# Fewer and larger weight loads, four selector and cast moves, and a permute on ScalarE in a fused attention and feed-forward kernel

## The chip, the cores and the metric

The kernel runs on one core of a Trainium2 chip. The metric is device time in microseconds (us): the median of repeated runs. Beside the runs there is one profiled execution, whose trace is read here. Engines are named as the profile names them: PE (TensorE matmul), PEld (its weight loads), DVE (VectorE), ACT (ScalarE), POOL (GpSimd), SP (SyncE). L145 is line 145 of the kernel.

## The reference

Inputs are q, k, v of shape [4 batches, 8 heads, 768 tokens, 64], a matrix `sort_net` [4, 8, 8, 8], and the weights of a feed-forward layer: w_in [512, 2048], w_out [2048, 512] and two scalars s and b. All are float32.

```
P = sort_net
repeat 5 times:                       # Sinkhorn
    P = exp(P - rowmax(P)); P = P / (rowsum(P)+1e-9); P = P / (colsum(P)+1e-9)
k_sorted[i] = sum_j P[i,j] * k[block j]     # 8 blocks of 96 tokens; the same for v
attn = softmax(q_block @ k_sorted_block^T / 8)
x    = attn @ v_sorted_block                # heads side by side: [3072, 512]
out  = (s * relu(x @ w_in)^2 + b) @ w_out
```

## The kernel before

The work goes batch by batch. The tokens of a batch are split into two halves of four blocks, so that eight tiles of 384 tokens pass through the feed-forward part: `ffn1` (L482, x @ w_in, 64 matmuls a tile, with relu on ACT and the square on DVE) and `ffn2` (L514, @ w_out). The order of every engine is written out by hand: the program is issued in one order, and `slots` of `ffn1` and `ffn2` name the attention pieces of the next batch that are issued between their matmuls. `k_piece` (L288) and `v_piece` (L372) mix the blocks with a matrix built from P. A k piece uses the loaded keys as weights. A v piece needs the values with token and feature dimension exchanged: `permute` (L184) writes them to the tile VP, [128, 64 features, 64], and a v piece reads 16 features of it.

**Start.** SP loads sort_net and batch 0's v as four float32 chunks `v0f` (L83). PE runs 160 matmuls on zeros, 110 columns wide (`warm`, L209). Meanwhile DVE and ACT run the Sinkhorn rounds (L210 to L225): exp on ACT, then a row sum, reciprocal, product, column sum, reciprocal, product on DVE (L216 to L224). Behind each exp from the second on, ACT casts and permutes one chunk of v0f into VP (L213), and in rounds 1 and 2 DVE fills its wait for the exp with a mask reduction (`idle`, L199). PE then spreads P over the partitions with the selector `emat` (`pe`, L236): GpSimd makes emat with a memset of all four batches (L131), a select for batch 0 (L132) and two for batches 1 to 3 (L172). For batch 0, DVE builds the mixing matrix `pd` (L255 to L268). For batches 1 to 3 the spread values are kept in PB, copied by ACT (L551). Three k pieces, four v pieces and the scores of batch 0 follow.

**GpSimd's queue.** All loads that change type are issued by GpSimd, in program order: batch 0's keys (L93) and the first half of its q tokens (L111), then `load_w` (L140). That one first copies one element of pd (L148), which makes the queue wait until pd is there, issues two parts of w_in, copies one element of the third key piece's result `ks` (L151) as a second gate, and issues the rest: 16 parts of w_in in all, each 128 rows by 512 columns, with the second half of q between them, and four parts of w_out (L165). Memsets follow (L580 to L586), then the two scalars (L588), and batch 1's loads: k and v in two halves each (`load_z`, L100) and q in eight parts. A load also waits until the load eight places before it has landed, since the two share a semaphore. Last come five copies of `permute` (L594), 8 features each, for features 0 to 39 of batch 1; DVE does features 40 to 63 in one copy, issued behind `make_bias` in slot 7 of `ffn1(1)` (L634).

**Where batch 1's values are used.** In `ffn2(0)` (L668), three k pieces stand in slot 2, three v pieces in slot 5 and the last in slot 9, all evicted by ACT and DVE in turn.

Of the kernel before, what the change touches and what calls it, by code (L numbers as in the profile page):

```python
# [12 lines left out]
ALU = mybir.AluOpType  # L13
# [3 lines left out]
def spread(t, dims):  # L17

    return bass.AP(tensor=t.tensor, offset=t.offset, ap=[list(t.ap[0])] + dims)
# [3 lines left out]
def kernel(  # L23
# [12 lines left out]
    nc = tc.nc  # L36

    B, H, S, D = q.shape
    NB = sort_net.shape[-1]
    BLK = S // NB  # L40
    BH = B * H
    NHP = H // 2
# [3 lines left out]
    HB = NB // 2  # L46
# [33 lines left out]
    v0f = gtp.tile([128, C2, D], FP, tag="gt", name="v0f")  # L80
    CV = C2 // 4
    for c in range(0, C2, CV):
        nc.sync.dma_start(out=v0f[:, c:c + CV, :].rearrange("p c d -> p (c d)"),  # L83
                          in_=raw[2][0][:, c * D:(c + CV) * D])

    RAW = {}
# [18 lines left out]
    def load_q(b, ns=range(NB)):  # L105

        if b not in QTOK:
            QTOK[b] = rawp.tile([BLK, NB, H, D], BF, tag="rawq", name="qtok")
        qv = q[b].rearrange("h (n t) d -> t n h d", n=NB)
        for n in ns:  # L110
            nc.gpsimd.dma_start(out=QTOK[b][:, n], in_=qv[:, n])  # L111
# [5 lines left out]
    KS = [const.tile([128, NG, 2, GAP], BF, name=f"ks{i}") for i in range(2)]  # L117
# [9 lines left out]
    ident = const.tile([128, 128], BF)  # L127
    make_identity(nc, ident)
    idv = ident.rearrange("p (a e j z) -> p a e j z", a=NHP, e=2, j=NB)
    emat = const.tile([BH, B, 128], FP)  # L130
    nc.gpsimd.memset(emat, 0.0)  # L131
    nc.gpsimd.affine_select(out=emat[:, 0], in_=emat[:, 0], pattern=[[-1, H], [0, 2 * NB]], base=0,  # L132
                            channel_multiplier=1, compare_op=ALU.not_equal, fill=1.0)
    load("k", 0, 3)
    load_q(0, range(HB))
    ones = const.tile([128, 32], BF)
    wi = const.tile([128, NHP, d_ff], BF)
    wo = const.tile([128, NF, d_model], BF)

    def load_w():  # L140
        wiv = moe_w_in.rearrange("(a p) f -> p a f", p=128)
        fq = d_ff // 4

        def part(a, f0, f1):
            nc.gpsimd.dma_start(out=wi[:, a, f0 * fq:f1 * fq], in_=wiv[:, a, f0 * fq:f1 * fq])  # L145


        nc.gpsimd.tensor_copy(out=ones[:, 0:1], in_=PD[0][:, 0, 0, 0:1])  # L148
        part(0, 0, 1)
        part(1, 0, 1)  # L150
        nc.gpsimd.tensor_copy(out=ones[:, 0:1], in_=KS[0][:, 0, 0, C2 - 1:C2])  # L151
        part(0, 1, 2)
        part(1, 1, 2)
        for c in (0, 1):
            for a in (2, 3):
                part(a, c, c + 1)
            if c == 0:
                load_q(0, range(HB, NB))
        for c in (2, 3):
            for a in range(NHP):  # L160
                part(a, c, c + 1)
        wov = moe_w_out.rearrange("(f p) n -> p f n", p=128)
        for c in range(4):
            fs = slice(c * (NF // 4), (c + 1) * (NF // 4))
            nc.gpsimd.dma_start(out=wo[:, fs, :], in_=wov[:, fs, :])  # L165
# [1 line left out]
    nc.gpsimd.memset(VS[0][:, :, D:VW], 1.0)  # L167
    nc.gpsimd.memset(VS[0][32:GAP, :, D:VW], 0.0)
    nc.gpsimd.memset(VS[0][32:C2, :, D:VW], 1.0)
    for z in range(2):  # L170
        em = emat[:, 1:B, z * 64:(z + 1) * 64]
        nc.gpsimd.affine_select(out=em, in_=em, pattern=[[-H, B - 1], [-1, H], [0, NB]], base=-H,  # L172
                                channel_multiplier=1, compare_op=ALU.not_equal, fill=1.0)
    Z = []

    def warm(n, w=512):
        for _ in range(n):
            if not Z:
                Z.append(psb.tile([128, 512], FP, tag="b", name="z"))
            nc.tensor.matmul(out=Z[0][:, 0:w], lhsT=zeros[:, 0:128], rhs=zeros[:, 0:w],  # L180
                             start=True, stop=True)


    def permute(eng, src, cs=slice(0, C2), ds=slice(0, D)):  # L184
        o, i = VP[:, ds, cs], src[:, cs, ds].rearrange("p c d -> p d c")
        if eng is nc.scalar:
            eng.copy(out=o, in_=i)  # L187
        else:
            eng.tensor_copy(out=o, in_=i)  # L189
# [11 lines left out]
            out=jsel, in_=ident.rearrange("p (h j z) -> p j h z", h=H, j=NB), axis=AX.XY, op=ALU.add),  # L201
        lambda: nc.vector.tensor_reduce(
            out=bm.rearrange("p (e z a) -> p e z a", e=2, z=2),
            in_=idv.rearrange("p a e j z -> p e z a j"), axis=AX.X, op=ALU.add),
    ]
    nc.vector.tensor_reduce(out=rstat, in_=sn, axis=AX.X, op=ALU.max)
    nc.vector.tensor_tensor(out=sn, in0=sn, in1=rstat.broadcast_to([BH, NB, NB]),
                            op=ALU.subtract)
    warm(160, 110)  # L209
    for it in range(5):  # L210
        nc.scalar.activation(out=sn, in_=sn, func=AF.Exp)
        if it >= 1:
            permute(nc.scalar, v0f, slice((it - 1) * CV, it * CV))  # L213
        if it in (1, 2):
            idle[it - 1]()
        nc.vector.tensor_reduce(out=rstat, in_=sn, axis=AX.X, op=ALU.add)  # L216
        nc.vector.reciprocal(out=rrec, in_=rstat)
        nc.vector.tensor_tensor(out=sn, in0=sn, in1=rrec.broadcast_to([BH, NB, NB]), op=ALU.mult)
        if it == 4:
            break  # L220
        nc.vector.tensor_reduce(out=rstat, in_=sne.rearrange("p i j -> p j i"),
                                axis=AX.X, op=ALU.add)
        nc.vector.reciprocal(out=rrec, in_=rstat)
        nc.vector.tensor_tensor(out=sn, in0=sn, in1=spread(rrec, [[0, NB], list(rrec.ap[1])]),  # L224
                                op=ALU.mult)  # L225

    PD = {}
    PT = const.tile([128, B, NB], FP)
    RC = const.tile([128, B], FP)
    PB = const.tile([128, B - 1, NB, NB], FP)  # L230
# [283 lines left out]
    def ffn2(t, slots):  # L514
        gt = GT.pop(t)
        last = t == 2 * B - 1
        for m in range(TG // 128 - int(last)):
            ops = psb.tile([128, d_model], FP, tag="b", name="ops")
            for f in range(NF):
                nc.tensor.matmul(out=ops, lhsT=gt[:, f, m * 128:(m + 1) * 128],  # L520
                                 rhs=wo[:, f, :], start=(f == 0), stop=(f == NF - 1))
                if f % 4 == 3:
                    if f == NF - 1:
                        store(t, m, ops)
                    for p in slots.get(m * 4 + f // 4, ()):
                        p()
        if last:
            m = TG // 128 - 1
            h = d_model // 4
            for n0, n in ((0, 2 * h), (2 * h, h), (3 * h, h)):  # L530
                ns = slice(n0, n0 + n)
                ops = psb.tile([128, n], FP, tag="b", name="ops")
                for f in range(NF):
                    nc.tensor.matmul(out=ops, lhsT=gt[:, f, m * 128:(m + 1) * 128],  # L534
                                     rhs=wo[:, f, ns], start=(f == 0), stop=(f == NF - 1))
                store(t, m, ops, ns)
# [11 lines left out]
    take_p(0, 1, spread_p(0, 1), jsel)  # L548
    build_pd(0)
    pe = spread_p(1, B - 1)  # L550
    nc.scalar.copy(out=PB, in_=pe)  # L551
    warm(3)
    k_piece(0, 0, "A")
    k_piece(0, CK, "D")
# [35 lines left out]
    load_z("k", 1)  # L590
    load_z("v", 1)
    load_q(1)
    for i in range(5):
        permute(nc.gpsimd, RAW["v", 1], ds=slice(i * 8, (i + 1) * 8))  # L594


# [56 lines left out]
    for b in range(B):  # L653
        n = b + 1
        if b:
            ffn1(2 * b, {0: [VR_(n, 0, "AD"), VR_(n, 1, "D")],
                         2: [VR_(n, 2, "AD"), lambda: v_back(n), load_qg(n)]} if n < B else {})
        if b:
            ffn1(2 * b + 1, {})
        if n < B:  # L660
            q_dma(n)
        if n == B:
            ffn2(2 * b, {})
            ffn2(2 * b + 1, {})
            break
        K3 = [K(n, 0, "A"), K(n, 1, "D"), K(n, 2, "A")]
        if n == 1:
            ffn2(2 * b, {2: K3,  # L668
                         5: [V(n, 0, "D"), V(n, 1, "A"), V(n, 2, "D"), load_vk(2)],
                         9: [V(n, 3, "D"), SC(n, 0, 0), SC(n, 0, 1)],  # L670
                         11: [P(n, 0, 0), SC(n, 0, 2), SC(n, 0, 3)]})
            ffn2(2 * b + 1, {0: [P(n, 0, 1)], 1: [P(n, 0, 2)],
                             2: [P(n, 0, 3), TD(n, 0), SC(n, 1, 0), SC(n, 1, 1)],
                             4: [P(n, 1, 0)], 5: [P(n, 1, 1), SC(n, 1, 2), SC(n, 1, 3)],
                             7: [P(n, 1, 2)], 8: [P(n, 1, 3), TD(n, 1)]})
        else:
            ffn2(2 * b, {2: K3, 7: [SC(n, 0, 0), SC(n, 0, 1)] + ([load_vk(3)] if n == 2 else []),
                         9: [SC(n, 0, 2), SC(n, 0, 3)]})
            ffn2(2 * b + 1, {0: [P(n, 0, 0), P(n, 0, 1)],
                             2: [P(n, 0, 2), P(n, 0, 3), TD(n, 0)],  # L680
                             3: [SC(n, 1, 0), SC(n, 1, 1)], 4: [SC(n, 1, 2), SC(n, 1, 3)],
                             6: [P(n, 1, 0), P(n, 1, 1)],
                             8: [P(n, 1, 2), P(n, 1, 3), TD(n, 1)]})
# [30 lines left out]
```

## Time and profile before

| what | us |
|---|---|
| median of 4 runs | 226.13 (225.97 to 226.39) |
| profiled execution, its own time | 227.47 |
| its span in the trace | 225.7 |
| PE busy | 217.2 |
| DVE busy, ACT busy, POOL busy | 111.7, 100.1, 60.2 |
| granted TensorE clock | 1.00 in every stage |

Line 1 of the page gives each engine's busy time. The chain is the work that ended last, followed back from the last instruction, at each step to what released it. In the timeline a line is: start, length, engine, line of code, operation, output<-inputs, shape, count; a bracket at its end is the engine's idle time before it and what ended it. In a table by stage (windows), the columns are the stretch and its length, the busy time of the chosen engine, the granted clock, the DMA engines' share and the GB/s that they moved.

Some rows that the next sections use (us):

| row | start | length |
|---|---|---|
| ACT cast of a v0f chunk, L187, four of them | 5.02, 6.63, 8.59, 10.60 | 1.55, 1.53, 1.51, 1.50 |
| ACT exp of the last round, L211 | 10.21 | 0.26 |
| ACT copy of PB, L551 | 12.43 | 0.32 |
| DVE pd, L268 | 12.67 | 0.35 |
| first key pieces on PE, L293 | 13.08 | 1.71 |
| first two key evictions by ACT, L282 | 13.82 | 2.03 |
| first w_in part issued, L145 | 13.65 | lands after 3.8 |
| GpSimd's eight w_in issues behind q | 21.58 | 4.70 |
| last w_out part issued, L165 | 32.27 | lands after 13.2 |
| batch 1's last v part issued, L100 | 41.76 | lands after 14.66 |
| DVE permute of batch 1, L189 | 56.51 | 1.18 |

### The profile page before, as it was taken

The page shows a single profiled execution, that of the slowest core. Times are in us where ns is not written, and L with a number is a line of the kernel's source. Part 1 is how long each engine was busy: PE and PEld are TensorE (multiplying, and loading weights), DVE is VectorE, ACT ScalarE, POOL GpSimd, SP SyncE. Part 2 cuts the span into 40 slices and gives each one's busy share as a digit, 9 for nine tenths or more (in the row PEclk, how much of TensorE's full clock was granted, in tenths as well). Part 3 has the DMA queues.
Part 4 walks back from the last instruction along what each step waited for, and adds up shares of the span by engine and source line. Part 5 has one row for each costly group of instructions (what it writes and reads, how often), then busy time and mean ns, then how long its engine had stood idle before and what let it go on. Part 6 is the DMA issues. An engine that isn't in the chain of part 4 may idle for free.

```text
span 225.7 us, 5487 instructions
## 1 busy us (share of the span) xinstructions
PE 217.2 (96%) x2360; PEld 128.8 (57%) x2360; DVE 111.7 (49%) x232; ACT 100.1 (44%) x131; POOL 60.2 (27%) x101
## 2 busy tenths in 40 slices
PE   8897999999799999999999999999999999999993
PEld 8885656655355555555545545656455566554453
DVE  6747467571746657443318556343425743441222
ACT  4977476565124506655351326664345046550000
POOL 8539679643940006400040009100000000000000
PEclk9999999999999999999999999999999999999999
DMA  5999999989989946997949859969913240001212
GB/s 174 251 104 121 140 178 180 201 181 150 122 179 220 213 125 126 153 120 163 231 94 189 217 163 132 158 63 210 189 77 78 104 119 0 1 0 49 93 46 93
DMA packets 66872, 30.51 MB, mean 135 GB/s; under 512 B 57568, under 2 KB 62048, under 8 KB 66656
## 3 DMA queue, kind: packets, MB, share of 16 engines
q0 software_dynamic: 30960, 12.85, 47.5%
q1 hardware_dynamic: 35888, 17.31, 32.4%
q8 instruction: 18, 0.29, 0.5%
q14 instruction: 6, 0.05, 0.1%
HBM read 29.63 MB, written 8.65 MB: 170 GB/s over the span
## 4 chain that ended last, share of the span: by engine, by line
PE 72%; DMA 11%; POOL 9%; issue 2%; ACT 2%; DVE 2%; SPq 0%; POOLq 0%
PE ops L520 34%; PE hps L495 28%; DMA rawv<-in_v_dram 6%; DMA wi<-in_moe_w_in_dram 3%; PE pv L439 3%; PE sc L404 2%; POOL qtok L111 2%; POOL VP L189 2%; PE tp L293 2%; DMA v0f<-in_v_dram 2%; PE ops L534 2%; POOL wi L145 1%; POOL wo L165 1%; ACT ks L282 1%; ACT VP L187 1%
## 5 line engine op out<-in xcount | busy, mean ns | idle before, releaser
L495 PE MATMUL hps<-xt,wi 128*128 128x384 bf16 x512 | 86.4, 326 | 0.3 <-DVE rec L446 0.3
L520 PE MATMUL ops<-wo,gt 128*128 128x512 bf16 x368 | 85.0, 380 | 0.0
L509 ACT ACTIVATE rt<-hps 128x768 bf16<-128x768 f32 x64 | 51.5, 810 | 51.6 <-PE hps L495 49.8
L495 PEld LDWEIGHTS <-wi 128*128 128x128 bf16 x512 | 48.9, 98 | 34.4 <-issue 2.1
L510 DVE TENSOR_TENSOR gt<-rt 128x768 bf16<-128x768 bf16 x64 | 35.5, 557 | 44.8 <-ACT rt L509 44.5
L520 PEld LDWEIGHTS <-gt 128*128 128x128 bf16 x368 | 34.0, 98 | 37.7 <-issue 0.6
L542 DVE SCALAR_TENSOR_TENSOR ot<-ops,s_bc,bias 128x512 f32<-128x512 f32 (+2 forms) x26 | 18.4, 708 | 35.4 <-PE ops L520 33.5
L409 ACT ACTIVATE at<-sc 96x768 bf16<-96x768 f32 (+1 forms) x28 | 21.3, 805 | 30.6 <-PE sc L404 30.6
L111 POOL DMA_DIRECT2D qtok<-in_q_dram x32 | 25.4, 816 | 9.9 <-issue 3.4
L447 DVE TENSOR_TENSOR x<-pv,rec 96x512 bf16<-96x512 f32 x32 | 22.0, 687 | 1.1
L439 PEld LDWEIGHTS <-at 112*128 112x128 bf16 (+3 forms) x256 | 11.5, 101 | 5.2 <-ACT vs L282 1.0
L439 PE MATMUL pv<-vs,at 112*128 112x66 bf16 (+3 forms) x256 | 12.4, 195 | 0.8 <-DVE vs L284 0.8
L180 PE MATMUL z<-zeros 128*128 128x110 bf16 (+1 forms) x166 | 11.7, 240 | 1.0 <-DVE zeros L114 1.0
L282 ACT CAST ks<-tp 128x1024 bf16<-128x1024 f32 x8 | 8.1, 1012 | 8.4 <-PE tp L293 8.4
L180 PEld LDWEIGHTS <-zeros 128*128 128x128 bf16 x166 | 10.1, 111 | 1.3 <-DVE zeros L114 1.0
L446 DVE RECIPROCAL rec<-pv 96x8 f32<-96x8 f32 x32 | 6.3, 198 | 9.0 <-PE pv L439 9.0
L649 POOL COPY gate<-gt 128x1 bf16<-128x1 bf16 x2 | 0.4, 189 | 36.6 <-DVE gt L510 36.6
L145 POOL DMA_DIRECT2D wi<-in_moe_w_in_dram x16 | 8.7, 561 | 2.7 <-DMA wi<-in_moe_w_in_dram 1.8
L284 DVE CAST ks<-tp 128x1024 bf16<-128x1024 f32 x4 | 4.9, 1227 | 6.0 <-PE tp L293 6.0
L404 PE MATMUL sc<-qt,ks 64*128 64x96 bf16 x224 | 7.5, 204 | 0.2 <-DVE x L447 0.2
L404 PEld LDWEIGHTS <-ks 64*128 64x128 bf16 x224 | 5.2, 94 | 3.9 <-issue 1.7
L293 PEld LDWEIGHTS <-rawk 128*64 128x64 bf16 x384 | 6.4, 113 | 1.7 <-issue 1.7
(97 smaller groups left out, 118.3 us busy)
## 6 DMA issues: line engine op xcount, KB each, us to landing
out_dram<-ot SPq DMA_DIRECT2D x23, 256.0 KB, 2.1
qtok<-in_q_dram POOLq DMA_DIRECT2D x32, 96.0 KB, 8.7
rawk<-in_k_dram POOLq DMA_DIRECT2D x6, 384.0 KB, 10.0
rawv<-in_v_dram POOLq DMA_DIRECT2D x6, 384.0 KB, 6.7
dv<-VO SPq DMA_DIRECT2D x12, 192.0 KB, 7.5
vs<-dv SPq DMA_DIRECT2D x2, 1152.0 KB, 7.4
wi<-in_moe_w_in_dram POOLq DMA_DIRECT2D x16, 128.0 KB, 6.0
wo<-in_moe_w_out_dram POOLq DMA_DIRECT2D x4, 512.0 KB, 10.4
```

The costliest lines, as they stand in the source:

```text
L111: nc.gpsimd.dma_start(out=QTOK[b][:, n], in_=qv[:, n])
L145: nc.gpsimd.dma_start(out=wi[:, a, f0 * fq:f1 * fq], in_=wiv[:, a, f0 * fq:f1 * fq])
L180: nc.tensor.matmul(out=Z[0][:, 0:w], lhsT=zeros[:, 0:128], rhs=zeros[:, 0:w], start=True, stop=True)
L404: nc.tensor.matmul(out=sc[:, e, n * BLK:(n + 1) * BLK], lhsT=KS[b % 2][pr, g0 + n].rearrange("p z c -> p (z c)"), rhs=QT[b][pr, half * HB ...
L409: nc.scalar.activation(out=at, in_=sc[0:rows(b), :, 0:TG], func=AF.Exp, scale=scale)
L439: nc.tensor.matmul(out=pv[0:m, e, n * VW:(n + 1) * VW], lhsT=atf[:, c0:c0 + m], rhs=VS[b > 1][:, e * NG + g0 + n, 0:VW], start=True, stop= ...
L447: nc.vector.tensor_tensor(out=x[:, :, hp * 128:(hp + 1) * 128].rearrange("p n (e d) -> p e n d", e=2), in0=pvv[:, :, :, 0:D], in1=rec.unsq ...
L495: nc.tensor.matmul(out=H1[i][:, f, 0:TG], lhsT=wi[:, hp, fc:fc + 128], rhs=xt[:, :, hp, :], start=(hp == 0), stop=(hp == NHP - 1))
L509: nc.scalar.activation(out=rt, in_=h, func=AF.Relu)
L510: nc.vector.tensor_tensor(out=gt[:, 2 * i:2 * i + 2, :], in0=rt, in1=rt, op=ALU.mult)
L520: nc.tensor.matmul(out=ops, lhsT=gt[:, f, m * 128:(m + 1) * 128], rhs=wo[:, f, :], start=(f == 0), stop=(f == NF - 1))
L542: nc.vector.scalar_tensor_tensor(out=ot[:, ns], in0=ops, scalar=s_bc, in1=BIAS[0][:, ns], op0=ALU.mult, op1=ALU.add)
```

## The change

w_in is loaded in 8 parts of two row blocks each instead of 16 of one. The first gate of `load_w` waits for the first key piece's eviction instead of pd; the order is now both column quarters 0 and 1 for all rows, then q, then quarters 2 and 3. The selector of batches 1 to 3 is made on DVE, from the identity, in the idle slots of Sinkhorn rounds 3 and 4, and GpSimd clears only batch 0's. The casts of the third and fourth v0f chunk come behind the last exp. PB is copied by DVE. The warm-up is 128 matmuls of 138 columns. Of batch 1's value permutes, GpSimd leaves out features 24 to 31, and ACT does these behind the three k pieces of `ffn2(0)`.

```diff
-    nc.gpsimd.memset(emat, 0.0)
+    nc.gpsimd.memset(emat[:, 0], 0.0)
...
-        def part(a, f0, f1):
-            nc.gpsimd.dma_start(out=wi[:, a, f0 * fq:f1 * fq], in_=wiv[:, a, f0 * fq:f1 * fq])
-        nc.gpsimd.tensor_copy(out=ones[:, 0:1], in_=PD[0][:, 0, 0, 0:1])
-        part(0, 0, 1)
-        part(1, 0, 1)
+        def part(a, f):
+            nc.gpsimd.dma_start(out=wi[:, a:a + 2, f * fq:(f + 1) * fq],
+                                in_=wiv[:, a:a + 2, f * fq:(f + 1) * fq])
+        nc.gpsimd.tensor_copy(out=ones[:, 0:1], in_=KS[0][:, 0, 0, 0:1])
+        part(0, 0)
         nc.gpsimd.tensor_copy(out=ones[:, 0:1], in_=KS[0][:, 0, 0, C2 - 1:C2])
-        part(0, 1, 2)
-        part(1, 1, 2)
-        for c in (0, 1):
-            for a in (2, 3):
-                part(a, c, c + 1)
-            if c == 0:
-                load_q(0, range(HB, NB))
-        for c in (2, 3):
-            for a in range(NHP):
-                part(a, c, c + 1)
+        part(0, 1)
+        part(2, 0)
+        part(2, 1)
+        load_q(0, range(HB, NB))
+        for f in (2, 3):
+            for a in (0, 2):
+                part(a, f)
...
-    for z in range(2):
-        em = emat[:, 1:B, z * 64:(z + 1) * 64]
-        nc.gpsimd.affine_select(out=em, in_=em, pattern=[[-H, B - 1], [-1, H], [0, NB]], base=-H,
-                                channel_multiplier=1, compare_op=ALU.not_equal, fill=1.0)
...
+    ] + [
+        lambda z=z: nc.vector.tensor_copy(
+            out=emat[:, 1:B, z * 64:(z + 1) * 64].rearrange("p b (h j) -> p b h j", h=H),
+            in_=ident[0:BH, H:B * H].rearrange("p (b h) -> p b h", b=B - 1).unsqueeze(3).broadcast_to(
+                [BH, B - 1, H, NB]))
+        for z in range(2)
     ]
...
-    warm(160, 110)
+    warm(128, 138)
     for it in range(5):
         nc.scalar.activation(out=sn, in_=sn, func=AF.Exp)
+        for c in {1: (0,), 2: (1,), 4: (2, 3)}.get(it, ()):
+            permute(nc.scalar, v0f, slice(c * CV, (c + 1) * CV))
         if it >= 1:
-            permute(nc.scalar, v0f, slice((it - 1) * CV, it * CV))
-        if it in (1, 2):
             idle[it - 1]()
...
-    nc.scalar.copy(out=PB, in_=pe)
+    nc.vector.tensor_copy(out=PB, in_=pe)
...
-    for i in range(5):
+    for i in (0, 1, 2, 4):
         permute(nc.gpsimd, RAW["v", 1], ds=slice(i * 8, (i + 1) * 8))
...
-            ffn2(2 * b, {2: K3,
+            ffn2(2 * b, {2: K3 + [lambda: permute(nc.scalar, RAW["v", 1], ds=slice(24, 32))],
```

## The prediction, made before the changed kernel was run

> **What bounds the kernel now.** I read the page's busy shares and its chain by engine first, then the chain of waits in order of time, then the timeline around the one place where TensorE stands still.
>
> ```profile
> PE 217.2 (96%) x2360; PEld 128.8 (57%) x2360; DVE 111.7 (49%) x232; ACT 100.1 (44%) x131; POOL 60.2 (27%) x101
> PE 72%; DMA 11%; POOL 9%; issue 2%; ACT 2%; DVE 2%; SPq 0%; POOLq 0%
> ```
>
> TensorE is busy 96% of the span, yet only 72% of the chain lies on it. 20% lies on DMA and GpSimd, and the chain in order of time says where:
>
> ```profile
> 15.97 0.19 POOL ones L151
> ...
> 22.67 7.11 DMA wi<-in_moe_w_in_dram
> ...
> 41.76 14.66 DMA rawv<-in_v_dram
> 56.41 0.28 issue
> 56.70 1.36 POOL qtok L111
> 58.06 3.94 POOL VP L189 x5
> 62.00 0.04 issue
> 62.04 0.70 PE tv L377 x32
> ```
>
> From 16 to 62 us the end is set by one queue: GpSimd's loads (w_in, q, w_out, then batch 1's k, v, q), the landing of batch 1's second v half at 56.41, GpSimd's last q issue, its five permutes. After 62.7 the chain holds nothing but TensorE until the last store, so what is won at 62 is won at the end. The timeline of TensorE shows how much can be won there:
>
> ```profile
> 55.99 2.76 PE L520 MATMUL ops<-wo,gt 128*128 128x512 bf16 x12
> 58.95 0.44 PE L377 MATMUL tv<-pd,VP 128*64 128x64 bf16 x16 [0.19 <-POOL VP L189]
> 59.73 0.44 PE L377 MATMUL tv<-pd,VP 128*64 128x64 bf16 x16 [0.35 <-POOL VP L189]
> 60.50 0.44 PE L377 MATMUL tv<-pd,VP 128*64 128x64 bf16 x16 [0.33 <-POOL VP L189]
> 61.28 0.44 PE L377 MATMUL tv<-pd,VP 128*64 128x64 bf16 x16 [0.34 <-POOL VP L189]
> 62.04 0.70 PE L377 MATMUL tv<-pd,VP 128*64 128x64 bf16 x32 [0.32 <-POOL VP L189]
> 62.67 3.63 PE L520 MATMUL ops<-wo,gt 128*128 128x512 bf16 x16
> ```
>
> Start to start, 32 tv matmuls take 0.63 us (62.04 to 62.67), so the 96 of them are 1.9 us of work. TensorE is ready at about 58.75 and goes on at 62.67: 3.9 us, of which 2.0 are waiting for permutes.
>
> **Selector on VectorE.** GpSimd loses two selects (0.98 us) and three quarters of a memset (0.51 to about 0.26, the 128x128 memset of sel): its k and q issues start 0.25 us earlier. TensorE does not wait for those landings, so that is worth nothing. But one of the selects stood beside a VectorE step of the Sinkhorn chain:
>
> ```profile
> 6.11 0.21 DVE L224 TENSOR_TENSOR sne<-sne,rrec 32x64 f32<-32x64 f32 x1
> 7.88 0.98 POOL L172 TENSOR_SCALAR_AFFINE_SELECT emat<-emat 32x192 f32<-32x192 f32 x2
> 8.01 0.39 DVE L224 TENSOR_TENSOR sne<-sne,rrec 32x64 f32<-32x64 f32 x1
> ```
>
> The same step took 0.21 elsewhere and 0.39 under the select, so -0.18 on the start-up chain. The two new copies (192 elements; nearest rows 0.27 for L202 and 0.35 for L255) go into VectorE's 0.32 us wait for the exp in rounds 3 and 4, as the two reduces of rounds 1 and 2 do now: 0. Without that cover they would cost up to 0.7.
>
> **Casts behind the last exp.** The last exp starts 0.03 after its input, so the move frees nothing now. ScalarE then has two casts (1.51, 1.50) behind the exp: 10.42 to 13.4 with the 0.18 taken off, and its next work, the first key eviction, is due at 13.64 (13.82 less 0.18). Margin 0.2. The copy of PB (0.32) would have used it up; it goes to VectorE behind pd, into a 1.30 us gap before 14.32 (row L255, 0.35). Both: 0. If the casts run over, each tenth is a tenth on the start-up chain. The first tv (14.88) needs all four casts, 1.3 us later.
>
> **Warm-up.** 160x110 = 17,600 columns against 128x138 = 17,664: 9.72 us become 9.76, ending 10.7, before pe at 11.33: 0. If a matmul cost the same whatever its width, the warm-up would end at 8.8; the granted clock is 1.00 in every row, so what a longer pause costs isn't shown. From both sides: 0, or at worst the key moves at twice their 1.71 us. I take 0, since columns fit. The program also gets 64 TensorE instructions shorter; TensorE's pause of 0.33 at 17.46, put down to issue, may vanish or fall elsewhere: plus or minus 0.4, value 0.
>
> **w_in in 8 parts, later.** GpSimd's issue cost: 16 x 0.56 = 9.0 before. A part of twice the rows lies between 0.56 (128 KB) and 0.76 (w_out, 512 KB); at 0.62, 8 x 0.62 = 5.0. That saving of 4 us and the 2.8 us of waits before w_in and w_out issues buy little by themselves, because the DMA engines behind the queue are full: what counts is when the queue has served everything ahead of v. Its rate by stage:
>
> ```profile
> 14.00:16.00 2.00, 0.84 (x3) 1.00 0.50 67
> 18.00:20.00 2.00, 2.00 (x4) 1.00 0.93 128
> 20.00:22.00 2.00, 2.00 (x4) 1.00 1.08 133
> 38.00:40.00 2.00, 2.00 (x3) 1.00 1.22 201
> ```
>
> The last column is GB/s: 67 to 133 while GpSimd hands out small parts, 201 when w_out is under way. Now the late side: the first gate waits for the first key eviction, which ends at 14.83 - 0.18, instead of pd; with the 0.13 and 0.45 us that the second gate shows before and after its copy, the first part is issued at 15.2 instead of 13.65, 1.6 later. Then the sum. An idle queue landed its first part 3.8 us after issue, so a part twice as large lands at 15.2 + 3.8 + 0.65 = 19.7 (w_out: 1.57 MB between landings at 37.7 and 45.5, so 0.65 per 128 KB). Three more parts at 1.3 (w_out's rate) to 2.0 (133 GB/s) each: 23.6 to 25.7. Four q parts at 0.62: 26.1 to 28.2. Before, the same bytes, q and both weight quarters, were in at 28.30 (22.13 plus 6.17). So batch 1's v, behind the same w_out, would land 0.1 to 2.2 earlier; I take 0.7, below the middle, because parts also landed far slower than 0.65 apart (at 26.86, 28.30 and 29.78) while the queue was full, and that may come again. Nothing in front is starved: q's second half was used at 27.5 (lands 24.3 to 28.2; a stall of at most 0.7 that the wait at 58.95 swallows, TensorE having slack up to there), the third weight quarter from 31.6.
>
> A rule that speaks against the larger parts: the Trainium skill, DMA: Bandwidth & Descriptors, Latency and other measured facts, has copies slow down from 214 to 164 GB/s as the row pitch in HBM grows to 2 MiB, and a part now reaches over two row blocks 1 MiB apart. w_out's parts, with four blocks 256 KB apart, show 201. By the rule (an estimate, 0.2 slower over 8 x 1.3 us) the queue would be 2 us later and the gain gone; by the row it is as above.
>
> **An eighth on ScalarE.** GpSimd's permutes go from five to four, spaced 0.78: -0.78. ScalarE's piece costs at most 0.76 (half of a 768-element cast of 1.52) behind the key evictions, which end at 57.1; ScalarE is idle for 4.66 us before 61.77, so 0. It waits for both v halves, and queued behind it is only that eviction.
>
> **The sum.** With v landing e earlier, GpSimd starts permuting at 58.05 - e and ends at 61.2 - e, and TensorE goes on 0.78 + e earlier, as long as TensorE itself is not the limit. That limit is 0.18 + 2.0 = 2.2. The 0.18 does not add to the first: it is contained in the gate's time. With e = 0.7: 1.5. The profiled execution took 227.47 (span 225.7 and 1.77 around it) and would take 226.0; the median of the runs, 226.13, lies 1.34 below it, and with the same 1.5 off it is **224.6 us**.
>
> **The rivals.**
> - The whole wait goes (e of 1.4 or more): 2.2 off, 223.9. For it: the underfilled stages before 22 us, and the top of my bounds. Against: the later gate.
> - The queue lands v when it did (e near 0): only the eighth counts, 0.8 off, 225.3. For it: the DMA share is high in every stage, so the bytes decide.
> - On the other side: the later gate is carried to the end. If the larger parts are served no faster than the small ones, the whole queue is 1.6 later, v lands at 58.0, e = -1.6, and TensorE goes on 0.8 later: 226.9. It decides from e below -0.8. For it: the stages at 92 to 133 GB/s may be the memory's pace and not GpSimd's.
> - The change doesn't do what it says: the casts push the first key eviction, which eats the 0.18 and moves the gate with it; worth some tenths inside the range.
>
> **How the numbers follow.** Forecast (e from 0.3 to 1.4) 0.40; whole wait gone 0.24; the eighth alone 0.18; queue later 0.15; something unforeseen at no change 0.03. Of the eighth alone 0.02, and of the later queue 0.06, lie within 0.2% of before, which is about what a measurement of this kernel can tell from no change. Faster: 0.40 + 0.24 + 0.16 = 0.80; same: 0.02 + 0.06 + 0.03 = 0.11; slower: 0.09. The range goes from 223.5 (2.2 off and the 0.4 of the issue pause) to 226.0 (e = -0.7), leaving out the slow end.
>
> **What would show it.** Right: the second v half lands before 56, four permutes of 0.8 end before 61, the idle time at tv with GpSimd as releaser falls from 1.5 us to under half, L224 is 0.21 in every round, and ScalarE's first key eviction starts near 13.6. Wrong: v landing after 57, a wait of TensorE for w_in or q between 25 and 32, a cast that ends after the first tp, or a warm-up that ends near 9.

## The result: no measurable difference

The changed kernel took 225.86 us (median of 36 runs, 224.34 to 228.08), the kernel before, run beside it, 225.97 (median of 55 runs, 224.53 to 229.22). The ratio is 0.9998 with a 95% interval of 0.9982 to 1.0014. The medians are of all runs; the ratio and its interval leave out the few runs that took over 1.5% longer than the fastest of their kernel. The forecast was 224.6. The profiled execution of the changed kernel took 227.55 us; its span is 225.8.

From the page after, the lines that answer to those of before (busy shares, granted clock by slices, chain by engine):

```profile
PE 218.5 (97%) x2328; PEld 129.1 (57%) x2328; DVE 115.5 (51%) x235; ACT 100.6 (45%) x131; POOL 54.4 (24%) x90
...
PEclk9999969999999999999999999999999999999999
...
PE 90%; DMA 4%; POOL 2%; ACT 1%; DVE 1%; issue 0%; POOLq 0%
```

The chain has changed as intended: GpSimd's share of it went from 9% to 2%, and DMA's from 11% to 4%. Yet the end has not moved. The 4% that are left on DMA are one piece in the chain in order of time (start, us, what):

```profile
20.53 8.75 DMA qtok<-in_q_dram
...
61.18 1.64 PE tv L376 x96
62.82 3.56 PE ops L519 x16
```

The timeline of TensorE has both places, the one that was to be mended (tv) and a new one. Before, the 16 transposes of q's second half (tqb) ran in one group:

```profile
27.48 0.85 PE L331 MATMUL tqb<-ident,qtok 96*128 96x96 bf16 x16
28.16 0.85 PE L495 MATMUL hps<-xt,wi 128*128 128x384 bf16 x4
```

After (start, us, engine, line, operation; in brackets the idle time before it and what ended it):

```profile
27.48 0.34 PE L330 MATMUL tqb<-ident,qtok 96*128 96x96 bf16 x4 [0.66 <-DMA qtok<-in_q_dram]
28.10 0.34 PE L330 MATMUL tqb<-ident,qtok 96*128 96x96 bf16 x4 [0.28 <-DMA qtok<-in_q_dram]
28.70 0.34 PE L330 MATMUL tqb<-ident,qtok 96*128 96x96 bf16 x4 [0.26 <-DMA qtok<-in_q_dram]
29.32 0.49 PE L330 MATMUL tqb<-ident,qtok 96*128 96x96 bf16 x4 [0.28 <-DMA qtok<-in_q_dram]
29.62 1.48 PE L494 MATMUL hps<-xt,wi 128*128 128x384 bf16 x4
...
61.11 1.71 PE L376 MATMUL tv<-pd,VP 128*64 128x64 bf16 x96
62.75 3.63 PE L519 MATMUL ops<-wo,gt 128*128 128x512 bf16 x16
```

At tv the wait is gone: the 96 matmuls run in one group of 1.64 us, start to start, where before they took 3.72 in five groups. But TensorE starts tv 2.16 later than before (61.11 against 58.95), although it was 0.82 ahead at its first w_in matmul (22.81 against 23.63). It now waits for q's second half ahead of each of the four groups of transposes, 1.48 us in all by the brackets. Before, the same 16 transposes went through, the first to the last starting from 27.48 to 28.11, with no wait. From the first w_out matmul behind tv on, both kernels take 163.0 us to the end, so all that differs lies ahead of that mark.

In this one execution a slower clock followed the waits. The windows of TensorE of two executions of the changed kernel (us, busy, granted clock, DMA share, GB/s), first the profiled one, then "after_again" below:

```profile
29.00:32.00 3.00, 2.72 (x20) 0.56 1.24 206
32.00:35.00 3.00, 3.00 (x29) 0.87 1.24 206
```

```profile
29.00:32.00 3.00, 2.76 (x29) 1.00 1.24 206
32.00:35.00 3.00, 3.00 (x44) 1.00 1.17 180
```

Both had waited for q just before (1.48 us and 1.10 by the brackets); the clock fell to 0.56 only in the first. That execution is 1.7 us longer than the kernel's median, and the stretch behind the waits (29.62 to the first w_out matmul) took 1.4 more than in the second. So the comparison below leans on several executions.

### The profile page after: what moved, and what is told of

The parts are those of the page before. It is cut to its first block, busy times and chain, and to the rows that moved or that the text cites. A ratio compares the mean times of both kernels' runs of the same rounds, so it can differ in the third digit from the quotient of the medians.

```text
span 225.8 us, 5414 instructions
## 1 busy us (share of the span) xinstructions
PE 218.5 (97%) x2328; PEld 129.1 (57%) x2328; DVE 115.5 (51%) x235; ACT 100.6 (45%) x131; POOL 54.4 (24%) x90
## 4 chain that ended last, share of the span: by engine, by line
PE 90%; DMA 4%; POOL 2%; ACT 1%; DVE 1%; issue 0%; POOLq 0%
PE ops L519 36%; PE hps L494 36%; PE z L173 5%; DMA qtok<-in_q_dram 4%; PE pv L438 3%; PE tp L292 2%; PE sc L403 2%; PE ops L533 2%; POOL wi L145 1%; POOL qtok L111 1%; PE tv L376 1%; PE vob L357 1%; PE scb L418 1%; PE pe L235 0%; ACT ks L281 0%
## 5 line engine op out<-in xcount | busy, mean ns | idle before, releaser
L494 PE MATMUL hps<-xt,wi 128*128 128x384 bf16 x512 | 87.7, 329 | 0.3 <-DVE rec L445 0.3
L494 PEld LDWEIGHTS <-wi 128*128 128x128 bf16 x512 | 49.4, 99 | 35.0 <-issue 3.2
L509 DVE TENSOR_TENSOR gt<-rt 128x768 bf16<-128x768 bf16 x64 | 38.8, 608 | 46.2 <-ACT rt L508 46.0
L111 POOL DMA_DIRECT2D qtok<-in_q_dram x32 | 24.7, 785 | 8.0 <-DMA wo<-in_moe_w_out_dram 4.7
L173 PE MATMUL z<-zeros 128*128 128x138 bf16 (+1 forms) x134 | 11.9, 258 | 1.2 <-DVE zeros L115 1.2
L292 PE MATMUL tp<-pd,rawk 128*64 128x64 bf16 x384 | 6.8, 196 | 0.0
```

What stands on the lines that cost most here:

```text
L292: nc.tensor.matmul(out=ps[e * 64:(e + 1) * 64, c].rearrange("p z g -> p (z g)"), lhsT=src[:, c0 + c, :], rhs=mov[:, e].rearrange("p z g -> ...
L494: nc.tensor.matmul(out=H1[i][:, f, 0:TG], lhsT=wi[:, hp, fc:fc + 128], rhs=xt[:, :, hp, :], start=(hp == 0), stop=(hp == NHP - 1))
L509: nc.vector.tensor_tensor(out=gt[:, 2 * i:2 * i + 2, :], in0=rt, in1=rt, op=ALU.mult)
```

## The experiments

The theory: the gain at tv is **traded** for the wait at tqb, since the changed order puts 1 MB of w_in ahead of q where 0.75 MB stood. The rivals named in the expectations: a wait at tv of 2.0 us in every execution, so that something larger must have been lost ("full wait"), and a wait for q that only the first profile had ("odd profile"). Each kernel ran in five rounds beside the kernel before. What lies ahead of the mark is read from two stretches of each trace: from the first tqb matmul to the first w_out matmul (24.19 us where nothing is lost), and from the first tv to the next w_out matmul (1.64 to 1.87 where nothing waits). They leave out the time up to the first tqb matmul, which starts anywhere from 26.78 (q_third) to 28.83 (all_but_loadw).

| kernel | median us | ratio to before (95%) | q's last part lands | tqb to w_out | tv to w_out | span |
|---|---|---|---|---|---|---|
| before, profiled | 225.97 | | 25.47 | 24.18 | 3.72 | 225.7 |
| before_again | 225.87 | 0.9996 (0.9971 to 1.002) | 27.88 | 25.09 | 2.66 | 224.8 |
| after, profiled | 225.86 | 0.9998 (0.9982 to 1.0014) | 29.28 | 26.61 | 1.64 | 225.8 |
| after_again | 225.71 | 0.9975 (0.995 to 0.9999) | 29.20 | 25.17 | 1.64 | 224.2 |
| only_loadw | 225.94 | 1.0003 (0.9974 to 1.0032) | 28.63 | 24.19 | 1.87 | 224.1 |
| only_eighth | 225.36 | 0.9983 (0.9959 to 1.0008) | 26.14 | 24.19 | 2.95 | 224.7 |
| start_only | 225.75 | 0.9994 (0.9969 to 1.002) | 26.26 | 24.19 | 2.33 | 223.9 |
| all_but_loadw | 225.20 | 0.9983 (0.9958 to 1.0009) | 25.58 | 24.19 | 1.87 | 224.7 |
| gate_pd | 226.20 | 0.9998 (0.9964 to 1.0033) | 29.70 | 25.35 | 1.64 | 224.7 |
| small_parts | 225.88 | 0.9996 (0.9962 to 1.003) | 28.49 | 24.95 | 2.09 | 223.9 |
| q_third | 225.25 | 0.9974 (0.9951 to 0.9998) | 26.59 | 24.19 | 1.87 | 222.7 |
| q_third_again | 225.44 | 0.9981 (0.9963 to 1.0) | 27.98 | 25.38 | 1.87 | 224.1 |
| gate_pd_q3 | 225.06 | 0.9952 (0.9928 to 0.9977) | 27.30 | 24.25 | 1.64 | 223.4 |
| gate_pd_q3_again | 224.70 | 0.9943 (0.9924 to 0.9963) | 26.27 | 24.19 | 1.87 | 223.2 |

**only_loadw**: the kernel before with the new order, gates and parts of w_in alone.

```diff
-        nc.gpsimd.tensor_copy(out=ones[:, 0:1], in_=PD[0][:, 0, 0, 0:1])
-        part(0, 0, 1)
-        part(1, 0, 1)
...
+        nc.gpsimd.tensor_copy(out=ones[:, 0:1], in_=KS[0][:, 0, 0, 0:1])
+        part(0, 0)
...
+        part(2, 0)
+        part(2, 1)
         load_q(0, range(HB, NB))
```

> The kernel before with only the new w_in loads: 8 parts, the first gate behind the first key eviction, q behind four of them. Theory 'traded' (the start-up became some 0.8 us shorter and the wait for q's second half at 27.5 us takes it back; the wait at tv is small in an ordinary execution): nothing is won at the start, q is late, so 226.3 to 227.0, slower than before by 0.3 to 1.0. Theory 'full wait' (the 2.0 us of waiting at tv stand in every execution and the new loads remove them, so that something larger must have been lost): 225.0 to 226.0, not slower.

No difference to before: 225.94 misses the 226.3 to 227.0 that "traded" expected and lies within the rival's 225.0 to 226.0, so this time does not speak for the theory. Its profile has no wait at tv, and v landed at 52.45, with five permutes still on GpSimd: there the new loads alone brought v early enough. q came late (28.63). In this execution it cost nothing on top, since TensorE reached tqb only at 28.24: it had stood still earlier, with no wait that the profile shows (the timeline of TensorE):

```profile
24.33 0.43 PE L436 MATMUL pv<-vs,at 112*128 112x66 bf16 x8 [1.56 <-issue]
```

**all_but_loadw**: the changed kernel with the diff of only_loadw reversed, so with the old loads of w_in. **only_eighth**: the kernel before with ScalarE's eighth alone, the diff below. **start_only**: all_but_loadw with this diff reversed, so with all five permutes on GpSimd.

```diff
-    for i in range(5):
+    for i in (0, 1, 2, 4):
         permute(nc.gpsimd, RAW["v", 1], ds=slice(i * 8, (i + 1) * 8))
...
-            ffn2(2 * b, {2: K3,
+            ffn2(2 * b, {2: K3 + [lambda: permute(nc.scalar, RAW["v", 1], ds=slice(24, 32))],
```

> The changed kernel with the old w_in loads (16 parts, old order and old gate). 'Traded': the start-up gain of about 0.8 us stays and q is there in time: 225.0 to 225.4. 'Full wait': the start-up gain and the eighth add up, 0.8 + 0.8: 224.4.

> The kernel before with only the permute of features 24 to 31 on ScalarE. 'Traded': the wait at tv is mostly absent in an ordinary execution: 225.7 to 226.0, no more than 0.3 faster. 'Full wait': the price of one permute, 0.78 off: 225.2.

> This is the changed kernel with the 16 small parts of w_in in their old order and gates, and all five permutes of batch 1's values on GpSimd: only the selector, the casts, the copy of PB and the warm-up are changed. Theory (what is won at the start is lost again at the wait of TensorE for batch 1's values, as the queue is not earlier by more than the gate's 0.3): first scores 0.5 to 0.8 earlier than before's 18.02, but tv's end at most 0.3 earlier than in the typical execution of before, so 225.6 to 226.0, ratio 0.998 to 1.000. Rival (start-up carried to the end): 0.8 off, about 225.2, ratio 0.9965.

The medians stand 0.71, 0.55 and 0.20 below before's of the same chip. The third is no difference that can be told, and the intervals of the first two reach just over 1. all_but_loadw and start_only came out as the theory expected; only_eighth, at 225.36, came nearer to the rival's 225.2 than to the 225.7 to 226.0 of "traded". In start_only the first scores started at 17.89, only 0.13 ahead of before's 18.02 where 0.5 to 0.8 was expected. The medians add up (0.55 and 0.20 make 0.75), but each interval is over 0.5 us wide to either side. So it is likely, and not shown, that start-up and eighth are worth some 0.7 together, the eighth most of it, and that the new loads take it back in the changed kernel.

**after_again** and **before_again**: both kernels unchanged, for a second profile each.

> The changed kernel once more, for a second profile and as the partner of the three others on this chip. 'Traded' (start-up shorter by some 0.5 to 0.8, the wait at tv gone, and what both win is taken back by TensorE waiting for q's second half before its transposes): q's last part lands at 28.5 or later and TensorE waits over 1 us for it in this profile too; 225.6 to 226.1. 'Odd profile' (the wait for q was that one execution's, and the ordinary one loses its time elsewhere): a wait for q under 0.4.

> The kernel before, unchanged, as a second profile. Theory (the profiled execution that the prediction summed on was an untypical one): span near 224.2 in place of 225.7, the wait at tv by 1 us or more shorter than 2.0, and batch 1's second v half landing before 56.0. Rival (the wait of 2.0 is typical): tv's five groups spread again over 3.5 us or more, v landing near 56.4, and the difference of the span comes from another place. Time 225.97 within 0.3 by either.

The changed kernel's median stood 0.53 below before's in this batch, with an interval that ends at 0.9999, and 0.11 below in the 36 runs: there may be a gain of a few tenths, and what can be said is that it is not the forecast's 1.5. The changed kernel waits at tqb again, 1.43 us more from the first group to the last than the 0.63 of an unstalled pass (27.32 to 29.38). In the second profile of before, TensorE's timeline shows a wait split in two:

```profile
28.73 0.66 PE L495 MATMUL hps<-xt,wi 128*128 128x384 bf16 x3 [0.20 <-DMA wi<-in_moe_w_in_dram]
...
36.62 0.99 PE L495 MATMUL hps<-xt,wi 128*128 128x384 bf16 x5 [0.48 <-DMA wi<-in_moe_w_in_dram]
...
59.30 1.47 PE L377 MATMUL tv<-pd,VP 128*64 128x64 bf16 x64
61.10 0.69 PE L377 MATMUL tv<-pd,VP 128*64 128x64 bf16 x32 [0.34 <-POOL VP L189]
```

TensorE lost 0.9 us to q and w_in between 27 and 37 (25.09 against 24.19 in the table) and was ready for tv 0.5 later, while v landed 1.0 earlier (55.43 against 56.41); so it lost 0.8 there (2.66 against 1.87) where the first profile lost 1.9. The wait that the prediction set out to save is not the same in every execution of before, and part of what is lost early is not lost again at tv. The span fell less than expected, to 224.8 and not 224.2.

**q_third** and **q_third_again**: the changed kernel with q's second half one part further ahead.

```diff
         part(2, 0)
-        part(2, 1)
         load_q(0, range(HB, NB))
+        part(2, 1)
```

> The changed kernel with q's second half moved up by one part of w_in, in front of part(2, 1). 'Traded': q lands 1.3 to 2 us earlier and TensorE no longer waits for it: 224.8 to 225.3, about 0.7 faster than before. 'Full wait': q's wait wasn't what took the gain, so it stays within 0.3 of the changed kernel: 225.6 to 226.1.

> The changed kernel with q's second half as third in the queue instead of fourth. Theory (q's wait is what takes the gain back): q lands 26.5 to 27.5, TensorE waits less than 0.7 at tqb, and the time is 0.5 to 0.9 below the changed kernel's 225.86, so 225.0 to 225.4, ratio to before 0.996 to 0.998. Rival (the first result of 225.25 was luck of the batch): 225.7 to 226.0, ratio 0.999 to 1.001.

The medians are 0.66 and 0.51 below before's of the same chip. That is more than the 0.11 of the changed kernel's 36 runs, but hardly beyond the 0.53 of after_again, and the second missed what was expected by a little. In the first profile tqb runs through (26.78 to 27.42), and 0.25 us of waiting for w_in follow. In the second, q landed at 27.98, and the part that now stands behind it came late as well (the timeline of TensorE):

```profile
28.03 0.34 PE L330 MATMUL tqb<-ident,qtok 96*128 96x96 bf16 x4 [0.28 <-DMA qtok<-in_q_dram]
29.33 0.82 PE L494 MATMUL hps<-xt,wi 128*128 128x384 bf16 x4 [0.95 <-DMA wi<-in_moe_w_in_dram]
```

So the order moves the wait more than it removes it while the queue as a whole starts late. That is what the next two ask.

**gate_pd**: the changed kernel with the first gate back on the copy of pd. **gate_pd_q3** and **gate_pd_q3_again**: that and q in third place.

```diff
-        nc.gpsimd.tensor_copy(out=ones[:, 0:1], in_=KS[0][:, 0, 0, 0:1])
+        nc.gpsimd.tensor_copy(out=ones[:, 0:1], in_=PD[0][:, 0, 0, 0:1])
         part(0, 0)
```

> The changed kernel with the first gate of the weight loads back on pd, so that the first part is issued about 1.6 us earlier; order and size of the parts stay. 'Traded': q's second half lands 0.6 to 1.3 us earlier, and the time falls by about as much: 224.9 to 225.4. 'Odd profile': no gain beyond 0.2 against the changed kernel.

> The early gate and q's second half in front of part(2, 1), both. 'Traded': either alone takes nearly all of the wait for q, so both together are within 0.3 of the better one: 224.8 to 225.3. 'Odd profile': as the changed kernel, within 0.3.

> The changed kernel with q's second half as third in the queue and the first gate back on the pd copy. Theory: q lands 27.0 to 27.5, hardly a wait at tqb, and with the earlier queue the values land early too: 225.0 to 225.2, ratio 0.995 to 0.9965, and below q_third by 0 to 0.3. Rival (the gate is worth nothing once q stands third): equal to q_third within 0.1.

The earlier gate alone wins nothing, where "traded" expected 224.9 to 225.4 and q 0.6 to 1.3 earlier: it moves up one part (13.52), the others still stand behind the second gate, and q landed at 29.70. With q third, the waits at tqb and tv go in both profiles; in the first, 0.35 us of waiting for w_in are left. The timeline of TensorE in gate_pd_q3_again:

```profile
27.31 0.84 PE L330 MATMUL tqb<-ident,qtok 96*128 96x96 bf16 x16
...
58.52 1.71 PE L376 MATMUL tv<-pd,VP 128*64 128x64 bf16 x96
60.39 3.40 PE L519 MATMUL ops<-wo,gt 128*128 128x512 bf16 x15 [0.16 <-issue]
```

This is the only version whose interval against before stays clearly below 1, twice (0.9952 and 0.9943; the second from 6 runs), 1.2 us faster than before, and the second result was better than expected. Between gate_pd and gate_pd_q3, on one chip, nothing differs but the order of two loads, and the ratios to before are 0.9998 and 0.9952, 1.0 us apart (the intervals touch between 0.9964 and 0.9977): the order makes the difference. Against the changed kernel itself it is 0.65 below after_again on the same chip; its second interval (up to 0.9963) lies clear of that of the changed kernel's 36 runs (from 0.9982), its first does not of after_again's.

**small_parts**: the changed kernel, each part split into its two row blocks, so 16 parts in the new order.

```diff
-            nc.gpsimd.dma_start(out=wi[:, a:a + 2, f * fq:(f + 1) * fq],
-                                in_=wiv[:, a:a + 2, f * fq:(f + 1) * fq])
+            for r in (a, a + 1):
+                nc.gpsimd.dma_start(out=wi[:, r, f * fq:(f + 1) * fq], in_=wiv[:, r, f * fq:(f + 1) * fq])
```

> The changed kernel with every part of w_in split into its two row blocks again: 16 small parts, the new order and the new gates. If the order and the gate make q late, and not the size: q lands as late as in the changed kernel, 225.6 to 226.2. If the large parts are served better or worse than small ones: over 0.3 away from the changed kernel, either way.

No difference to before or to the changed kernel; q lands at 28.49 and waits remain at tqb. So the size of the parts is not what brings q late. In all five profiles with 1 MB of w_in ahead of q it landed at 28.49 to 29.70, in the four with 0.75 MB in large parts at 26.27 to 27.98.

The traces tell more, since each load is reported by 16 DMA engines one by one. The median engine had q's last part at 27.0 to 27.5 in the five profiles with 1 MB ahead, and at 24.9 to 26.3 in the nine others: that is what the order moves. The last engine, which counts, came 0.3 to 2.7 us behind the median one, in either order (0.3 in before, 2.5 in before_again, 2.2 in after).

## Why the prediction was wrong

**The step that failed first** is the one on q: "a stall of at most 0.7 that the wait at 58.95 swallows". Two things were wrong in it. Its size: q's last part was put at 26.1 to 28.2 and landed at 29.28 and 29.20. The working took the first part's landing at 19.7 (it was 19.64) and then parts at 1.3 to 2.0; the second landed only 4.1 later, at 23.70, and q's parts waited behind it. The median of the 16 DMA engines had the second part at 21.63 and q's last at 27.1, within the sum's bounds; the last engine was 2.1 and 2.2 behind. That lag is a term that the sum on q left out; with q in before it was only 0.3. The page's list of DMA issues between 14 and 36 us shows q's delay as the time from issue to landing (last column, median us), before and after:

```profile
qtok<-in_q_dram POOLq DMA_DIRECT2D x4, 96.0 KB, 4.9
```

```profile
qtok<-in_q_dram POOLq DMA_DIRECT2D x4, 96.0 KB, 9.0
```

And its cover: the wait at 58.95 can swallow a stall only as long as it is there. The same sum spends it on the earlier v and the eighth; as v came even earlier than taken, nothing of it was left at tv, and the stall counted in full. The stretch from tqb to w_out grew by 1.0 in after_again (25.17 against 24.19), and by 2.4 in the profiled execution, whose further 1.4 goes with the fallen clock; ahead of it stand 0.22 and 0.66 us more of waiting for q.

**The step that failed second** is the base: a gain read on an execution of 227.47 was taken off the median of 226.13. That execution stands 1.5 above the median of the 55 runs, with the longer wait at tv of the two profiles and a pause of 0.33 at 17.46. Where hardly a wait is left (gate_pd_q3 in two batches), the medians are 225.06 and 224.70, 1.2 below before. So 1.2 is about what removing the waits is worth in a median execution, not the limit of 2.2. Of the forecast's 1.5 the base accounts for some 0.3; the changed kernel's order and gate, which left 0.1 (36 runs) to 0.5 (after_again) of the 1.2, for the larger part. Taken off the profiled execution itself, the forecast's 1.5 would have given 226.0.

**What held.** v landed at 53.45 and 55.00 instead of 56.41 (before_again: 55.43), so e, put at 0.7, was 0.4 to 3.0, and the wait at tv is gone in both profiles. The permutes on GpSimd went from 3.94 to 3.15, 0.79 less, as worked out; the eighth alone gave 0.55 in the medians, below 0.78, which fits a wait that is often shorter than the profiled one, though 0.78 lies within its interval as well. The row after:

```profile
54.51 3.15 POOL L182 COPY VP<-rawv 128x384 bf16<-128x384 bf16 x4
```

L223, the old L224, takes 0.21 in every round: the 0.39 is gone. The casts end at 12.98, before the first key eviction at 13.52; the warm-up's z rows end at 11.07; PB on VectorE costs nothing. But the start of pe varies from 11.01 to 11.69 between profiles with the new start-up, and from 11.33 to 11.79 with the old, so 0.18 can't be seen in times. A part cost 0.71 to issue, not 0.62; nobody waited for that.

**The rule on the row pitch** (the Trainium skill, DMA: Bandwidth & Descriptors, Latency and other measured facts) does not bear on this change as the prediction took it: the page's figures (207 GB/s at 512 KiB, 164 at 2 MiB, 214 at full rate) are for the pitch from one partition's row to the next, and w_in's rows lie 8 KiB apart from partition to partition in both kernels. No slow-down was seen either: parts with two blocks 1 MiB apart landed 1.3 apart, and the DMA engines moved 206 GB/s from 29 to 35 us.

**Of the rivals**, the one on the other side had the later gate in it, but carried by v, which came early; it was q that paid. No rival named q; among the signs of being wrong, the wait for q between 25 and 32 did.

**Left open.** Why the last DMA engine lags 2 us in one execution and 0.3 in another, and what made the clock fall in one execution of two alike. Whether the early gate is needed beside the order: with it the medians are 225.06 and 224.70, without it 225.25 and 225.44, but the intervals overlap.

## What to carry to other kernels

A wait at the end of a queue covers stalls ahead of it. Who removes it has to price these stalls anew, from the landing of every load in the queue and not only of the one in question: moving bytes ahead of a load is an edit to that load. The landing is set by the last DMA engine, so one execution's landing is not yet a price. And a gain that is a wait should be read from two or more executions, since part of it is only the luck of the one that was profiled; here the loss at tv was 1.9 in one and 0.8 in the other.

## What the runs showed of the hardware

- TensorE paused with no wait that the profile shows: 1.56 us at 24.33 in only_loadw, and in all_but_loadw

```profile
18.67 0.26 PE L406 MATMUL sc<-qt,ks 64*128 64x96 bf16 x4 [1.09 <-issue]
```

 The trace shows transfers of the instruction queue, which share the DMA engines with the loads, starting 2.5 us ahead of each (21.82 and 16.24). That TensorE waits for its instructions there fits, but was not tested, and transfers of that queue at 22.31 in q_third and 22.66 in after_again have no such pause behind them. Two executions of one kernel differ in it: before has 0.33 at 17.46, before_again none there.
- The clock fell to 0.56 after four waits none of which was over 0.66 us by its row. The Trainium skill (TensorE: Matmul & The Clock Gate, Why this matters for your kernels) tells to keep idle gaps under about 3 us; these were far shorter, and such waits in after_again (1.10 us in all) and gate_pd (1.70) left the clock at 1.00. It fell a second time in all_but_loadw, behind the pause of 1.09 (windows of TensorE, as above):

```profile
20.00:23.00 3.00, 2.35 (x39) 0.68 1.40 135
23.00:26.00 3.00, 2.81 (x30) 0.75 1.83 169
```

- A load is in when the last of 16 DMA engines has reported. For q's last part after, the median engine was done at 27.1 and the last at 29.28, and TensorE's last group of tqb started at 29.32: 2.2 us that the mean GB/s of the queue doesn't show.
